# Attention scores of all head pairs laid end to end in 13 groups of 1024 columns

## The chip, the core and the metric

The kernel runs on one core of a Trainium2 chip. The metric is device time in microseconds. Three runs of the kernel before took 338.5, 338.7 and 338.97 us (median 338.7). A profile is one further execution; its durations are those of single instructions, and an average over a group of them is called a mean.

## The reference

Causal attention with 16 extra keys and values ("beacons") that every query sees, and behind it a two-layer network with ELU, over all 4608 tokens:

```python
# q, k, v: (8, 8, 576, 64); beacon_k, beacon_v: (8, 8, 16, 64)
k_all = concat([beacon_k, k], axis=2)              # 592 keys
v_all = concat([beacon_v, v], axis=2)
scores = (1/8) * q @ k_all.T                       # keys past the query are masked out
a = exp(scores - max); a /= a.sum(-1)
x = (a @ v_all) -> (8*576, 8*64)                   # tokens x 512
h = x @ w_in                                       # 512 x 2048
g = where(h > 0, h, exp(min(h, 0)) - 1)
out = g @ w_out                                    # 2048 x 512
```

## The kernel before

**Layout.** A batch has 8 heads, held as 4 pairs: the two heads of a pair lie on the two halves of the 128 partitions, so their score matmuls (64 rows each) run side by side in the array. Scores are computed transposed: keys on partitions, in five chunks of 128 (the last has 80), queries along the columns. A chunk keeps only the queries that may see it, from `ilo = [0, 112, 240, 368, 496]` on, so a pair has 576 + 464 + 336 + 208 + 80 = 1664 columns (`ECOLS`). No maximum is subtracted.

**Steps of attention.** All work is written as small functions, called "steps", which `run` calls in the order of one long text, `word.argument.argument`. Each engine takes its instructions in just that order; waits between engines come from the tiles that instructions read and write.

- `S.b.p.g` (line 302): scores of batch b, pair p, group g of 416 columns, into a PSUM tile of two banks, one per head. Four groups per pair.
- `x.b.p.g` (line 312): exponential of that group on ScalarE into the f16 tile `et` of the pair (2 x 1664 columns, six buffers).
- `m.b.p.g` (line 329): VectorE multiplies the triangles on the chunk's diagonal in that group by the 0/1 tile `triu`. Per pair of a batch from 1 on that is one of 224 columns, three of 256 and one of 160 on 80 partitions.
- `D.b.p.n` (line 360): in batches 3 to 7, VectorE adds the key chunks 1 to 4 of a pair up, so that row sums need fewer matmuls.
- `L.b.g` (lines 344 and 374): row sums of half g (pairs 2g and 2g+1), by matmuls with a matrix of ones; four heads at once, each on 32 columns of the array.
- `n.b.g` (lines 406 and 409): 1/sum on ScalarE as exp(-ln(sum)).
- `W.b.g.half` (line 344): products with v; a head's 64 values are made as two halves of 32, each half in its own PSUM tile (576 columns).
- `M.b.g.half` (line 441): VectorE scales a tile of products by 1/sum and writes it to the f16 tile `xT` of the 512 tokens that it belongs to, in two pieces where a batch crosses a tile of tokens.

Batch 0 is done in two parts of its queries (`A`: 256, `B`: the rest), by lines of its own (450, 457).

**Steps of the network.** `F` is x @ w_in (line 477), `e`/`u`/`k` or `e`/`r`/`g` are the ELU (lines 487, 492, 502; 487, 509, 515), `G` and `Q` are the second product (line 524; from the third tile of tokens on line 588, by seven products of quarters in place of eight, with `Z`, `J`, `wt` as its sums), and for the last two tiles of tokens `P`, `K`, `E`, `U`, `V`, `H`, `X` do most of the first product in the same manner (line 658).

**PSUM.** Its eight banks are split in three: `ops` (two tiles of one bank, second product), `hps` (two of one bank, first product) and `S` (two tiles of two banks). All of `S`, `L`, `W` and the transposes `T` of batches 1 and 2 take turns on the two `S` tiles. A tile is free for the next step when its last reader is done.

**Loads.** GpSimd (POOL) issues all loads with a change of type: `lq` (q and k of batches 0 to 2, transposed by `T` on TensorE), `lk` (q or k of batches 3 to 7 to DRAM in bf16; `lt` brings them back transposed, from SyncE's queue), `lv` (v), `wi`, `wo` (weights). `lp` fills the beacon keys. Output rows are stored from SyncE's queue by `s` and `J`.

**Warm-up.** `warm.12` and `wm.n` are matmuls on zeros (lines 207 and 214), 12 of 512 columns and 99 of 128, put between the steps of batch 0.

The tile that holds scores, and the one that holds sums or products, in the code before:

```python
s = sc[b, p, g] = psum.tile([P, 2, 512], FP32, tag="S", name="sc")       # S, 416 of 512 used
t = psum.tile([P, 1024], FP32, tag="S", name=name)[:, 512 - QA:512 - QA + S]   # L, and each half of W
```

with `QA` = 112, the queries that see the first key chunk alone.

Of the kernel before, what the change touches and what calls it, by code (L numbers as in the profile page):

```python
# [8 lines left out]
FP32 = mybir.dt.float32  # L9
FP16 = mybir.dt.float16  # L10
BF16 = mybir.dt.bfloat16
AFT = mybir.ActivationFunctionType
# [5 lines left out]
def kernel(  # L18
# [169 lines left out]
    triu = konst.tile([P, 2, P], FP16)  # L188
# [42 lines left out]
    tps, qkT, sc, ets = {}, {}, {}, {}  # L231
# [5 lines left out]
    @step  # L237
    def tri():
        nc.gpsimd.memset(triu, 1.0)
        nc.gpsimd.affine_select(  # L240
            out=triu, in_=triu, compare_op=ALU.is_ge, fill=0.0, base=0,
            pattern=[[0, 2], [1, P]], channel_multiplier=-1,
        )
# [28 lines left out]
    @step  # L272
    def cb(b, p):
        qkT[b, p] = qks[p]
        src = bkT[:, p, NB * b:NB * (b + 1)]
        nc.vector.tensor_tensor(out=qkT[b, p][:, 1, 0:NB], in0=src, in1=src, op=ALU.max)
# [14 lines left out]
    def S_(b, p, g):  # L291
        if (b, p) not in ets:
            ets[b, p] = attn.tile([P, 2, ECOLS], FP16, tag="et", bufs=6, name="et")
        s = sc[b, p, g] = psum.tile([P, 2, 512], FP32, tag="S", name="sc")
        t = qkT[b, p]
        c0, c1 = GW * g, GW * (g + 1)
        for (j, qa, qe, col) in lays[b]:
            a, e = max(c0, col), min(c1, col + qe - qa)
            if a >= e:
                continue  # L300
            for h in range(2):
                nc.tensor.matmul(  # L302
                    out=s[:, h, a - c0:e - c0],
                    lhsT=t[D * h:D * (h + 1), 1, P * j:P * (j + 1)],
                    rhs=t[D * h:D * (h + 1), 0, NB + qa + a - col:NB + qa + e - col],
                    start=True, stop=True, skip_group_check=True,
                )
    op["S"] = S_

    @step  # L310
    def x(b, p, g):
        nc.scalar.activation(  # L312
            out=ets[b, p][:, :, GW * g:GW * (g + 1)], in_=sc[b, p, g][:, :, 0:GW],
            func=AFT.Exp, bias=0.0, scale=SCALE)

    @step
    def m(b, p, g, eng="v"):

        c0, c1 = GW * g, GW * (g + 1)
        for (j, qa, qe, col) in lays[b]:  # L320
            base = NB if j == 0 else 0
            e = min(qe, ilo[j] + P - base)
            a, e = max(qa, qa + c0 - col), min(e, qa + c1 - col)
            if a >= e:
                continue
            t0 = a - ilo[j] + base
            o = ets[b, p][0:kc[j], :, col + a - qa:col + e - qa]
            if eng == "v":
                nc.vector.tensor_tensor(out=o, in0=o, in1=triu[0:kc[j], :, t0:t0 + e - a], op=ALU.mult)  # L329
            else:  # L330
                nc.gpsimd.affine_select(
                    out=o, in_=o, compare_op=ALU.is_ge, fill=0.0, base=t0,
                    pattern=[[0, 2], [1, e - a]], channel_multiplier=-1)

    def quad(b, g, qa, qe, t, half, first):
# [5 lines left out]
        for n, (j, a, e, c) in enumerate(pcs):  # L341
            for i in range(4):
# [4 lines left out]
                    rhs=ets[b, p][0:kc[j], i % 2, c:c + e - a],  # L347
# [5 lines left out]
    def D_(b, p, n, eng="v"):  # L353

        r_ = presum[b, p] = qks[p % 2].bitcast(FP16)[:, :, 0:S]
        t = ets[b, p]
# [7 lines left out]
    lt, ut, rls = {}, {}, {}  # L364
    QA = ilo[1]

    def quads(b, g, half, name):

        t = psum.tile([P, 1024], FP32, tag="S", name=name)[:, 512 - QA:512 - QA + S]
        if half is None and b >= BD:  # L370
            for a, e in ((0, QA), (QA, S)):
                for i in range(4):
                    k = b, 2 * g + i // 2
                    nc.tensor.matmul(
                        out=t[32 * i:32 * (i + 1), a:e], lhsT=ones,
                        rhs=(presum if a else ets)[k][:, i % 2, a:e],
                        start=True, stop=True, skip_group_check=True)
            return t
        quad(b, g, 0, QA, t[:, 0:QA], half, True)
        quad(b, g, QA, S, t[:, QA:S], half, True)  # L380
        return t

    @step
    def L(b, g):
# [7 lines left out]
        elif g == "B":  # L392
            t = psum.tile([P, 2, 512], FP32, tag="S", name="lt")
            for i in range(2):
                quad(b, i, CUT, S, t[:, i, 0:S - CUT], None, True)
            lt[b, g] = t[:, :, 0:S - CUT]
        else:
            lt[b, g] = quads(b, g, None, "lt")
# [21 lines left out]
    def W(b, g, *i):  # L420
        half = i[-1]
# [9 lines left out]
        else:  # L431
            ut[b, g, half] = quads(b, g, half, "ut")

    def scale_out(b, cc, qa, qe, u, r):

        tok, end = b * S + qa, b * S + qe
        while tok < end:
            k = tok // TT
            to = min(TT * (k + 1), end)
            o = tok - b * S - qa  # L440
            nc.vector.tensor_tensor(  # L441
                out=x_tile(k)[:, cc, tok - TT * k:to - TT * k],
                in0=u[:, o:o + to - tok], in1=r[:, o:o + to - tok], op=ALU.mult)
# [3 lines left out]
    def M(b, g, *i):  # L447
# [12 lines left out]
        else:  # L460
            scale_out(b, 2 * g + i[0], 0, S, ut[b, g, i[0]], rls[b, g][:, 0:S])
# [262 lines left out]
    def lt_(b, x_):  # L724
# [6 lines left out]
        for y in range(2):  # L731
            qkT[b, 2 * x_ + y] = t[:, y, :, :]
# [20 lines left out]
    lq.0.0.0.4 warm.12 lq.0.1.0.4 lq.0.0.4.8 ident wm.27 bt wm.6 T.0.0.0 bk cq.0.0.0 cb.0.2  # L753
    cb.0.1 T.0.1.0 ck.0.1.0 wm.10 S.0.1.0 x.0.1.0 wm.6 T.0.1.1 cb.0.0 ck.0.1.1 T.0.0.1 S.0.0.0
    x.0.0.0 wm.3 S.0.1.1 x.0.1.1 cq.0.0.1 wm.3 T.0.3.0 T.0.2.0 cb.0.3 cq.0.3.0 cq.0.2.0 S.0.0.1
    x.0.0.1 S.0.1.3 x.0.1.3 wm.8 S.0.1.2 x.0.1.2 lq.0.1.4.8 T.0.3.1 S.0.3.0 T.0.2.1 cq.0.3.1
    lq.1.0.0.4 lv.0.0.1 lv.0.2 tri m.0.1.3 x.0.3.0 cq.0.2.1 m.0.3.0 cb.1.1 S.0.0.3 x.0.0.3 wm.6
    S.0.3.3 x.0.3.3 wm.8 S.0.2.0 x.0.2.0 wm.4 S.0.2.2 wm.6 S.0.2.3 x.0.2.2 x.0.2.3 wm.6 S.0.3.2
    x.0.3.2 wm.6 S.0.0.2 x.0.0.2 wi.0 m.0.3.3 m.0.1.0 m.0.0.0 m.0.0.3 m.0.2.0 L.0.A n.0.A
    T.1.0.0 cb.1.0 m.0.3.2 cq.1.0.0 m.0.0.2 W.0.A.0 S.0.2.1 x.0.2.1 W.0.A.1 m.0.2.2 M.0.A.1  # L760
    M.0.A.0 cb.1.2 m.0.2.3 m.0.1.2 S.1.0.2 x.1.0.2 S.0.3.1 x.0.3.1 T.1.1.0 ck.1.1.0 S.1.0.0
    F.0.1 x.1.0.0 S.1.1.0 x.1.1.0 e.0.1 r.0.1 cb.1.3 g.0.1 F.0.3 S.1.0.3 x.1.0.3 L.0.B n.0.B
    lv.0.3.4 lq.1.0.4.8 wi.1 wo.0 W.0.B.0 M.0.B.0 S.1.1.3 e.0.3 u.0.3 x.1.1.3 F.0.0 u.0.0 e.0.0
    W.0.B.1 M.0.B.1 S.1.1.1 x.1.1.1 F.0.2 e.0.2 r.0.2 k.0.0 g.0.2 S.1.0.1 x.1.0.1 S.1.1.2
    x.1.1.2 F.1.1 u.1.1 lq.2.0.0.8 T.1.2.0 ck.1.2.0 e.1.1 T.1.3.0 F.1.4 e.1.4 k.0.3 cq.1.3.0
    r.1.4 g.1.4 m.1.1.2 cb.2.0 S.1.2.0 x.1.2.0 F.1.5 e.1.5 r.1.5 g.1.5 k.1.1 cb.2.1 S.1.2.2
    x.1.2.2 S.1.3.2 x.1.3.2 G.0.0.0 S.1.2.3 x.1.2.3 F.0.7 e.0.7 r.0.7 g.0.7 m.1.0.3 S.1.3.3
    x.1.3.3 S.1.2.1 x.1.2.1 F.0.4 e.0.4 G.0.1.0 S.1.3.0 x.1.3.0 F.0.5 e.0.5 r.0.4 m.1.3.2 g.0.4
    m.1.0.0 r.0.5 cb.2.2 T.2.2.0 ck.2.2.0 T.2.0.0 cq.2.0.0 m.1.2.0 g.0.5 F.1.7 S.2.2.0 x.2.2.0
    e.1.7 r.1.7 m.1.3.0 g.1.7 m.1.0.1 wo.1 G.0.1.1 S.1.3.1 x.1.3.1 S.2.2.2 x.2.2.2 F.1.0 e.1.0  # L770
    u.1.0 T.2.1.0 cq.2.1.0 m.1.0.2 m.1.1.3 m.1.1.1 wt.1.0 m.1.3.3 m.1.1.0 m.1.2.2 m.1.2.3
    m.1.3.1 m.1.2.1 T.2.3.0 ck.2.3.0 F.1.6 e.1.6 G.0.0.1 S.2.0.0 x.2.0.0 S.2.0.1 x.2.0.1 u.1.6
    m.2.2.2 k.1.6 cb.2.3 F.0.6 e.0.6 r.0.6 g.0.6 L.1.0 n.1.0 L.1.1 n.1.1 F.1.3 lv.1.2.3.4 wo.2
    lv.2.2.3.4 lv.1.0.1 W.1.0.1 M.1.0.1 W.1.0.0 M.1.0.0 k.1.0 F.1.2 e.1.2 u.1.3 u.1.2 e.1.3
    W.1.1.0 W.1.1.1 m.2.2.0 M.1.1.0 M.1.1.1 k.1.2 lk.3.0 G.0.0.2 S.2.0.3 x.2.0.3 S.2.0.2 x.2.0.2
    F.2.1 u.2.1 e.2.1 G.0.1.2 S.2.3.0 x.2.3.0 S.2.1.0 x.2.1.0 F.2.11 u.2.11 e.2.11 F.2.13
    S.2.1.2 x.2.1.2 S.2.3.1 x.2.3.1 wo.3 wt.1.1 lp.3.1 k.1.3 G.0.0.3 k.2.11 o.0.0 e.2.13 u.2.13
    k.2.13 H.1.1 F.2.15 u.2.15 e.2.15 S.2.1.1 x.2.1.1 S.2.3.3 H.1.0 G.0.1.3 o.0.1 k.2.15 m.2.0.0
    k.2.1 F.2.5 G.1.0.0 e.2.5 x.2.3.3 F.2.7 u.2.7 e.2.7 k.2.7 S.2.1.3 x.2.1.3 S.2.3.2 u.2.5
    x.2.3.2 G.1.1.0 F.2.3 G.1.0.1 e.2.3 r.2.3 S.2.2.3 x.2.2.3 S.2.2.1 x.2.2.1 g.2.3 m.2.0.1  # L780
    m.2.0.2 m.2.3.2 G.1.1.1 F.2.6 u.2.6 F.2.0 e.2.6 k.2.6 m.2.1.3 m.2.2.1 m.2.1.2 u.2.0 m.2.2.3
    m.2.1.1 m.2.3.0 m.2.0.3 k.2.5 m.2.1.0 lk.3.1 lt.3.0 s.0.0 lk.4.0 lv.3.0.1 lv.2.0.1 lp.3.0
    S.3.0.1 S.3.0.0 x.3.0.1 m.3.0.1 m.2.3.1 m.2.3.3 e.2.0 k.2.0 F.2.14 u.2.14 x.3.0.0 G.1.1.2
    F.2.8 e.2.8 e.2.14 G.1.0.2 S.3.0.3 x.3.0.3 S.3.0.2 x.3.0.2 wt.3.0 r.2.8 g.2.8 F.2.9 L.2.1
    n.2.1 W.2.1.1 M.2.1.1 D.3.0.0 F.2.2 u.2.2 e.2.2 W.2.1.0 M.2.1.0 e.2.9 r.2.9 g.2.9 m.3.0.0
    k.2.2 L.2.0 F.2.4 W.2.0.0 n.2.0 M.2.0.0 e.2.4 u.2.4 W.2.0.1 F.2.10 u.2.10 e.2.10 k.2.14
# [130 lines left out]
```

## Time and profile before

| | |
|---|---|
| profiled execution | 338.69 us, of which the span from first to last instruction is 337.0 |
| TensorE clock | 1.000 of full speed |
| line 477, first product | 544 matmuls, busy 119.4 us |
| line 588, second product | 896 matmuls, busy 50.6 + 50.0 + 17.3 us |
| line 312, exponentials | 128 of 128x832, busy 108.4 us, mean 916 ns |
| line 329, masks | 164, busy 37.7 us, mean 267 ns |
| line 441, scaling of products | 56, busy 22.4 us, mean 450 ns |
| lines 406 and 409, 1/sum | 14 each of 576 columns, mean 666 and 686 ns |

A group's busy time counts each moment once, also where its instructions overlap; its mean is the whole duration of one instruction, which starts before the one ahead of it has ended. So busy time divided by the count is less than the mean. Matmuls overlap most: the distance between starts tells more than their duration. In the lists of waits a line reads: engine, line, what it waited for, microseconds in all, times, longest. In the chain of waits and the timeline a line begins with start and length in microseconds, and ends with the number of instructions.

### The profile page before, as it was taken

Reading aid. Unit: us, or ns where it says so; the run is one execution under the profiler, and the core shown is the slowest. Engines: PE = TensorE matmul, PEld = TensorE weight load, DVE = VectorE, ACT = ScalarE, POOL = GpSimd, SP = SyncE. Lnnn points to the kernel's source line nnn. Section 1 sums busy time; section 2 is a strip of 40 time slices with the busy share of each in tenths; the row PEclk is TensorE's granted clock in tenths of the full one; section 3 lists DMA queues with packets and bytes.
Section 4 is the critical chain, followed back from the end, with each engine's and each line's share of the span. In section 5 each row is a group of like instructions: output and inputs, shape, how many; then the busy total and the mean of one; then the engine's idle time right before and its main releaser. Section 6 shows DMA issues by size and latency. Waiting matters only on the chain.

```text
span 337.0 us, 8983 instructions
## 1 busy us (share of the span) xinstructions
PE 329.2 (98%) x3643; PEld 210.8 (63%) x3643; DVE 286.0 (85%) x663; ACT 282.7 (84%) x474; POOL 91.2 (27%) x120
## 2 busy tenths in 40 slices
PE   8989999999999999999999999999999999999995
PEld 4767666444545556656565555555656688788684
DVE  2583898666899998999899889999999999999972
ACT  1899989799899988889698989997998688888840
POOL 8786468572015008052411300050000000000000
PEclk9999999999999999999999999999999999999999
DMA  9999999999949909989693914298100110121122
GB/s 115 180 162 189 201 185 166 160 173 154 166 33 126 120 2 110 163 150 144 67 142 84 138 33 107 58 109 68 64 3 31 33 64 31 33 94 33 57 70 93
DMA packets 129082, 34.66 MB, mean 103 GB/s; under 512 B 112913, under 2 KB 127505, under 8 KB 129041
## 3 DMA queue, kind: packets, MB, share of 16 engines
q0 software_dynamic: 94912, 18.49, 67.9%
q1 hardware_dynamic: 33408, 15.34, 21.8%
q8 instruction: 28, 0.46, 0.6%
q10 hardware_dynamic: 720, 0.26, 0.3%
q14 instruction: 14, 0.11, 0.1%
HBM read 37.22 MB, written 15.34 MB: 156 GB/s over the span
## 4 chain that ended last, share of the span: by engine, by line
PE 65%; DVE 20%; ACT 10%; issue 2%; DMA 1%; DVEq 0%; ACTq 0%
PE hps L477 21%; PE ops L588 21%; PE sc L302 6%; DVE gt L502 5%; PE hps L658 5%; ACT et L312 4%; PE ops L524 4%; PE ut L344 4%; DVE xT L441 3%; DVE qk L360 3%; DVE gt L545 2%; DVE et L329 2%; PE w L207 1%; DMA out_dram<-osb 1%; ACT e L487 1%
## 5 line engine op out<-in xcount | busy, mean ns | idle before, releaser
L477 PE MATMUL hps<-xT,w_in 128*128 128x512 f16 (+1 forms) x544 | 119.4, 355 | 0.5
L312 ACT ACTIVATE et<-sc 128x832 f16<-128x832 f32 x128 | 108.4, 916 | 7.1 <-PE sc L302 6.7
L588 PEld LDWEIGHTS <-gt 128*128 128x128 f16 x768 | 73.5, 98 | 19.7 <-issue 2.9
L502 DVE SCALAR_TENSOR_TENSOR gt<-e,r 128x512 f16<-128x512 f32 x108 | 72.9, 685 | 8.9 <-ACT e L487 6.3
L487 ACT ACTIVATE e<-hps 128x512 f32<-128x512 f32 x120 | 74.1, 637 | 6.1 <-PE hps L477 5.5
L477 PEld LDWEIGHTS <-w_in 128*128 128x128 f16 x544 | 49.0, 98 | 44.6 <-issue 8.0
L492 ACT ACTIVATE r<-hps 128x512 f16<-128x512 f32 x108 | 66.9, 637 | 7.1 <-PE hps L477 5.7
L588 PE MATMUL ops<-wt,gt 128*128 128x256 f16 x384 | 50.6, 273 | 0.5 <-DVE osb L604 0.5
L588 PE MATMUL ops<-w_out,gt 128*128 128x256 f16 x384 | 50.0, 273 | 0.0
L329 DVE TENSOR_TENSOR et<-et,triu 128x256 f16<-128x256 f16 (+3 forms) x164 | 37.7, 267 | 3.2 <-ACT et L312 3.2
L149 POOL DMA_DIRECT2D v<-in_v_dram x40 | 34.2, 871 | 12.4 <-issue 7.9
L545 DVE TENSOR_TENSOR gt<-gt 128x1024 f16<-128x1024 f16 x48 | 32.3, 686 | 0.4
L441 DVE TENSOR_TENSOR xT<-ut,rl 128x448 f16<-128x448 f32 (+7 forms) x56 | 22.4, 450 | 4.0 <-PE ut L344 2.8
L344 PEld LDWEIGHTS <-v 128*32 128x32 f16 (+1 forms) x800 | 17.2, 96 | 11.6 <-issue 2.5
L344 PE MATMUL ut<-et,v 128*32 128x464 f16 (+4 forms) x672 | 23.7, 282 | 0.1
L360 DVE TENSOR_TENSOR qk<-qk,et 128x672 f16<-128x672 f16 (+2 forms) x60 | 21.4, 368 | 0.6
L604 DVE TENSOR_TENSOR osb<-ops,sm 128x512 f32<-128x512 f32 x24 | 16.5, 685 | 4.2 <-issue 3.2
L588 PE MATMUL ops<-w_out,s 128*128 128x256 f16 x128 | 17.3, 273 | 0.0
L697 DVE SCALAR_TENSOR_TENSOR gt<-e,r 128x512 f16<-128x512 f32 x24 | 16.1, 686 | 0.6 <-ACT r L687 0.3
L524 PE MATMUL ops<-w_out,gt 128*128 128x512 f16 x64 | 16.5, 380 | 0.0
L588 PEld LDWEIGHTS <-s 128*128 128x128 f16 x128 | 12.4, 98 | 3.2 <-issue 0.2
L509 DVE SCALAR_TENSOR_TENSOR r<-e,one 128x512 f16<-128x512 f32 x12 | 8.3, 690 | 6.9 <-ACT e L487 6.9
(108 smaller groups left out, 395.0 us busy)
## 6 DMA issues: line engine op xcount, KB each, us to landing
out_dram<-osb SPq DMA_DIRECT2D x35, 256.0 KB, 2.2
v<-in_v_dram POOLq DMA_DIRECT2D x24, 128.0 KB, 7.5
scr<-in_q_dram POOLq DMA_DIRECT2D x5, 576.0 KB, 10.0
scr<-in_k_dram POOLq DMA_DIRECT2D x5, 576.0 KB, 14.5
w_in<-in_moe_w_in_dram POOLq DMA_DIRECT2D x16, 128.0 KB, 6.4
w_out<-in_moe_w_out_dram POOLq DMA_DIRECT2D x4, 512.0 KB, 11.4
v<-in_v_dram POOLq DMA_DIRECT2D x8, 112.0 KB, 6.2
v<-in_v_dram POOLq DMA_DIRECT2D x8, 80.0 KB, 6.7
```

The lines of the kernel that those rows point to most:

```text
L149: nc.gpsimd.dma_start(out=vt[b][r0:r0 + n, j, :, :], in_=v[b, :, ilo[j]:ilo[j] + n, :].rearrange("h s d -> s h d"),)
L312: nc.scalar.activation(out=ets[b, p][:, :, GW * g:GW * (g + 1)], in_=sc[b, p, g][:, :, 0:GW], func=AFT.Exp, bias=0.0, scale=SCALE)
L329: nc.vector.tensor_tensor(out=o, in0=o, in1=triu[0:kc[j], :, t0:t0 + e - a], op=ALU.mult)
L344: nc.tensor.matmul(out=t[32 * i:32 * (i + 1), a - qa:e - qa], lhsT=ones[0:kc[j], :] if half is None else v16[0:kc[j], j, h, 32 * half:32 * ...
L360: (nc.vector if eng == "v" else nc.gpsimd).tensor_tensor(out=o, in0=t[0:rows, :, a:e] if n == 0 else o, in1=t[0:rows, :, col:col + e - a], ...
L441: nc.vector.tensor_tensor(out=x_tile(k)[:, cc, tok - TT * k:to - TT * k], in0=u[:, o:o + to - tok], in1=r[:, o:o + to - tok], op=ALU.mult)
L477: nc.tensor.matmul(out=h[:, n_, :], lhsT=w_in16[:, cc, P * fc:P * (fc + 1)], rhs=xt[k][:, cc, a - TT * k:e - TT * k], start=(cc == 0), sto ...
L487: nc.scalar.activation(out=eb[t, i], in_=flat(hp[t, i]), func=AFT.Exp, bias=0.0, scale=1.0)
L492: nc.scalar.activation(out=rb[t, i], in_=flat(hp[t, i]), func=AFT.Relu, bias=0.0, scale=1.0)
L502: nc.vector.scalar_tensor_tensor(out=half(t, i), in0=eb[t, i], scalar=1.0, in1=rb[t, i], op0=ALU.subtract, op1=ALU.min)
L545: (nc.vector if eng == "v" else nc.gpsimd).tensor_tensor(out=o_, in0=a_, in1=b_, op=op_)
L588: nc.tensor.matmul(out=xy[t, n_][:, qd, :], lhsT=lw[:, P * qd:P * (qd + 1)], rhs=wt_[:, c, :], start=(first and qd == 0 and c == 0), stop= ...
```

## The change

For batches 1 to 7 the scores of the four pairs are laid end to end, 4 x 1664 = 6656 columns, and cut in 13 groups of 512 columns per head (1024 with both heads) that pay no heed to where a pair or a key chunk ends. `S.b.g` and `x.b.g` take the place of `S.b.p.g` and `x.b.p.g`; a group may need two pairs' q and k. `et` holds two pairs (three buffers in place of six), and the one group that crosses from the first two pairs to the last two has two exponentials of 512 columns (256 of each head), the others have one of 1024. Batch 0 keeps its groups of 416.

Masks of batches 1 to 7 are two steps per pair in place of four, with three multiplications in place of five: the triangles of chunks 0 and 1 together, those of 2 and 3 together, and that of chunk 4. `triu` gets a third plane for chunk 0, and is read with a stride of zero over the two heads.

In `L` the tile of row sums also takes the products with v of the first 112 queries, both halves. `W.b.g` then makes the other 464 columns of both halves in one tile. `M.b.g.0` scales the first 112 columns of both halves, `M.b.g.1` the rest.

The order text is another from beginning to end (1493 words in place of 1605; warm-up matmuls of 128 columns: 65 in place of 99).

```diff
-    triu = konst.tile([P, 2, P], FP16)
+    triu = konst.tile([P, 3, P], FP16)
...
+        for a, e, base in ((0, 1, NB), (1, 3, 0)):
+            nc.gpsimd.affine_select(
+                out=triu[:, a:e, :], in_=triu[:, a:e, :], compare_op=ALU.is_ge, fill=0.0, base=base,
+                pattern=[[0, e - a], [1, P]], channel_multiplier=-1,
+            )
...
+    EC2 = 2 * ECOLS
+    def et(b, p):
+        if (b, p // 2) not in ets:
+            ets[b, p // 2] = attn.tile([P, 2, EC2], FP16, tag="et", bufs=3, name="et")
+        return ets[b, p // 2][:, :, ECOLS * (p % 2):ECOLS * (p % 2 + 1)]
+    def span(b, g):
+        return (GW * g[1] + ECOLS * g[0], GW) if b == 0 else (512 * g[0], 512)
+    def S_(b, *g):
+        s = sc[b, g] = psum.tile([P, 2, 512], FP32, tag="S", name="sc")
+        c0, w = span(b, g)
+        c1 = c0 + w
+        for p in range(NP):
+            t = qk_of(b, p)
+            for (j, qa, qe, col) in lays[b]:
+                col += ECOLS * p
+                a, e = max(c0, col), min(c1, col + qe - qa)
+                if a >= e:
+                    continue
...
     def x(b, *g):
+        c0, w = span(b, g)
+        for d in range(NP // 2):
+            a, e = max(c0, EC2 * d), min(c0 + w, EC2 * (d + 1))
+            if a < e:
+                et(b, 2 * d)
+                nc.scalar.activation(
+                    out=ets[b, d][:, :, a - EC2 * d:e - EC2 * d], in_=sc[b, g][:, :, a - c0:e - c0],
+                    func=AFT.Exp, bias=0.0, scale=SCALE)
...
+    def m(b, p, g):
+        t = et(b, p)
+        if b > 0:
+            m_ = lambda c: triu[:, c:c + 2, :].unsqueeze(1).broadcast_to([P, 2, 2, P])
+            if g == 0:
+                mask(t[:, :, 0:2 * C1].rearrange("p h (j c) -> p h j c", j=2)[:, :, :, 0:P], m_(0))
+            else:
+                n_ = C3 - C2
+                mask(t[:, :, C2 - n_ + P:C3 + P].rearrange("p h (j c) -> p h j c", j=2)[:, :, :, n_ - P:n_], m_(1))
+                mask(t[0:kc[4], :, C4:ECOLS], triu[0:kc[4], 1:3, 0:ECOLS - C4])
+            return
...
     def L(b, g):
...
-            lt[b, g] = quads(b, g, None, "lt")
+            t = hd[b, g] = psum.tile([P, 1024], FP32, tag="S", name="lt")
+            r_ = lt[b, g] = t[:, 512 - QA:512 - QA + S]
...
+            quad(b, g, 0, QA, r_[:, 0:QA], None, True)
+            for half in range(2):
+                quad(b, g, 0, QA, t[:, 512 - QA * (3 - half):512 - QA * (2 - half)], half, True)
...
     def W(b, g, *i):
...
-            ut[b, g, half] = quads(b, g, half, "ut")
+            t = ut[b, g] = psum.tile([P, 2, 512], FP32, tag="S", name="ut")
+            for half in range(2):
+                quad(b, g, QA, S, t[:, half, 0:S - QA], half, True)
...
     def M(b, g, *i):
...
-            scale_out(b, 2 * g + i[0], 0, S, ut[b, g, i[0]], rls[b, g][:, 0:S])
+            if i[0] == 0:
+                scale_out(b, g, 0, QA, hd[b, g][:, 512 - 3 * QA:512 - QA].rearrange("p (h q) -> p h q", h=2))
+            else:
+                scale_out(b, g, QA, S, ut[b, g][:, :, 0:S - QA])
...
     run("""
-    lq.0.0.0.4 warm.12 lq.0.1.0.4 lq.0.0.4.8 ident wm.27 bt wm.6 T.0.0.0 bk cq.0.0.0 cb.0.2
-    cb.0.1 T.0.1.0 ck.0.1.0 wm.10 S.0.1.0 x.0.1.0 wm.6 T.0.1.1 cb.0.0 ck.0.1.1 T.0.0.1 S.0.0.0
...
+    warm.12 lq.0.0.0.4 lq.0.1.0.4 ident bt bk cb.0.3 T.0.1.0 wm.7 T.0.0.0 ck.0.1.0 lq.0.0.4.8
+    cb.0.1 S.0.1.0 wm.8 T.0.1.1 cq.0.0.0 cb.0.0 T.0.0.1 x.0.1.0 tri lq.0.1.4.8 ck.0.1.1 S.0.0.0
...
+    wo.3 W.1.1 F.1.6 u.1.3 wo.2 G.0.1.2 M.1.1.1 lk.3.0 e.1.6 u.1.6 S.2.8 S.2.6 x.2.8 x.2.6 k.1.3
...
+    k.4.0 D.4.3.3 F.4.11 F.4.8 S.5.3 x.5.3 W.4.0 D.4.2.3 L.4.1 Q.3.56.63 J.3.2.v Q.3.63.70
...
```

## The prediction

> **What bounds the kernel now.** First the page's head, with the busy times.
>
> ```profile
> span 337.0 us, 8983 instructions
> PE 329.2 (98%) x3643; PEld 210.8 (63%) x3643; DVE 286.0 (85%) x663; ACT 282.7 (84%) x474; POOL 91.2 (27%) x120
> ```
>
> TensorE (PE) is busy 98% of the span, but a busy PE need not stream at its rate, so I looked at the distances between its matmuls: first the chain of work that ended last, in order of time, where TensorE runs undisturbed, then the timeline of TensorE where it changes work.
>
> ```profile
> 151.27 1.53 PE ops L588 x14
> 152.80 0.86 PE hps L477 x4
> 154.42 1.73 PE hps L477 x8
> ```
> ```profile
> 109.22 0.93 PE L588 MATMUL ops<-wt,gt 128*128 128x256 f16 x7
> 110.08 0.53 PE L302 MATMUL sc<-kst 64*128 64x128 bf16 x10
> 110.54 1.04 PE L477 MATMUL hps<-xT,w_in 128*128 128x512 f16 x4
> 111.41 0.82 PE L588 MATMUL ops<-wt,gt 128*128 128x256 f16 x6
> ```
>
> Undisturbed, 256 columns take 1.53/14 = 0.109 us and 512 take 1.73/8 = 0.216, or 0.42 ns a column. In the second fence, seven matmuls from 109.22 should hand over at 109.98; the scores start at 110.08, 0.10 late. The ten score matmuls are two groups of 416 columns with both heads at once, 2 x 0.173 us, over at 110.43; line 477 starts at 110.54, 0.11 late. From line 477 to line 588 nothing is lost (110.54 + 0.86 = 111.40). So a change between tile shapes of the array (64 rows for scores, 32 columns for row sums and products with v, 64 columns for transposes, the whole array for the rest) costs about 0.10 us, and a change of work inside one shape costs nothing.
>
> Counting neighbours of different shape among the TensorE words of the order list gives 207 changes, or 207 x 0.102 = 21.1 us. Columns of all forms times 0.42 ns (512 columns 480 times, 256 columns 1192 times, scores 32 x 1664 with two heads at once, sums and products 69,000 with four at once, transposes) give 290 us, and the warm-up matmuls 10.5. With 1.3 us before the first matmul and 4.3 after the last one's start, some 10 of the 337.0 us are left for waiting, about half of them in the first 30 us. TensorE is the bound, and only fewer changes of shape, an earlier start or those waits can give time back.
>
> The waits and two windows say how near the other engines are.
>
> ```profile
> ACT et L312 <- PE sc L302: 6.7, 9, 1.6
> DVE et L329 <- ACT et L312: 3.2, 5, 1.0
> DVE osb L604 <- issue: 3.2, 1, 3.2
> ```
> ```profile
> 100.00:120.00 20.00, 20.00 (x180) 11.96 (x181) 19.79 (x49) 20.00 (x36) 5.61 (x9) 1.00 1.28 104
> 240.00:280.00 40.00, 40.00 (x404) 27.97 (x403) 39.79 (x93) 32.30 (x58) 0.00 (x0) 1.00 0.12 41
> ```
>
> Columns are window, length, busy PE, PEld, DVE, ACT, POOL, clock, DMA share, GB/s. VectorE (DVE) has no room from 240 to 280 us, and DVE and ScalarE (ACT) none from 100 to 120. TensorE still streams there, so they are just fast enough.
>
> In the first 30 us the chain names ScalarE:
>
> ```profile
> 6.14 1.51 PE w L214 x27
> 9.58 0.36 PE sc L302 x5
> 13.14 8.44 ACT et L312 x11
> 25.47 0.98 PE hps L477 x8
> ```
>
> The first score at 9.58 starts a row of exponentials, and line 477 begins at 25.47 because of them.
>
> **The change part by part.** The profiled run took 338.69 us, 1.69 more than its span; the median of the runs is 338.7, so sums against one hold for the other.
>
> *Changes of shape.* Batches 1 to 7 have 91 score groups in place of 112, and products with v are one word per half (14 in place of 28). The new order list, counted the same way, has 180 changes: 56 from full array to scores in place of 67, 58 back in place of 70, 12 to products in place of 22. 27 x 0.102 = 2.75 us saved. Every one lies on the bounding engine. Columns stay the same (1664 per pair, 464 + 112 per product).
>
> *Score pieces.* 13 groups a batch still make 32 pieces a batch, but three are 16, 48 and 32 columns wide. The narrowest row is 80 columns (line 344, 80x80), handed over after 33 ns like its columns. Bounds: nothing, or 33 ns for each short piece, 7 x (3 x 33 - 40) = 0.4 us. I take 0.2, the middle, as no row is that narrow. The Trainium skill, "TensorE: Matmul & The Clock Gate", section "Wait — 56ns, not 53.3ns?", says that starts never come closer than about 25 ns however few the columns; by that, as an estimate, the sum would have 7 x (75 - 40) = 0.25 us, and no run here shows it.
>
> *Exponentials.* From 832 to 1152 columns line 312 and the copies of line 280 go from 900 to 1131 ns less a fixed part, about 0.8 ns a column. In a row 13 take 10.12 us in the timeline (0.78 each, from 11.47), so 1024 columns take some 0.93 to 1.07. Per batch: 16 x 0.78 = 12.5 before; 12 x 0.94 and 2 x 0.51 (the group that crosses the two tiles) = 12.3 after. ScalarE saves 1 to 3 us, off the path but for the stretches above.
>
> *Masks.* 140 multiplications become 84: two of 512 columns and one of 160 per pair, in place of 224, three of 256 and 160. At line 329's busy mean of 37.7/164 = 0.23 us, 140 are 32 us. Line 641 has 128x512 f16 at 0.42 us; so 56 x 0.42 + 28 x 0.2 = 29 us, or less in a row. If the broadcast mask halved the rate, line 515's 0.69 us for 512 columns applies: 56 x 0.27 = 15 us more. I take the saving, 3 us: innermost the mask still steps through 128 neighbouring columns, as in line 329's own rows. Cover: TensorE's stream. Without it, 12 us more on VectorE.
>
> *Scaling of the products.* Forms of line 441 go from 284 ns (128 columns) to 620 (448): 1.05 ns a column and 0.15 fixed. 56 instructions become 42 with the same columns: 0.5 to 2.1 us less on VectorE, covered in the same way.
>
> *PSUM tiles.* Per half, three tiles of the ring of two that scores use become two, and 21 groups fall away: 154 allocations in batches 1 to 7 become 91 + 28 = 119. Against that, the tile with the sums now also holds the products of the first 112 columns: it is free only after line 409 (0.69 us) and a scaling on VectorE (224 columns, about 0.38), where line 406 freed it before. Queued behind a score group that waits for it are all later matmuls. Bounds: no wait, or 14 x 1.1 = 15 us. I take zero, since between line 374 at 220.88 and the next score at 222.82 the old order already left 1.9 us, about what the new hold needs.
>
> *Start.* The 27 warm-up matmuls ahead of the first beacon transpose go (1.5 us of the chain), and the identity is built ahead of the third pair of loads. The first transpose needs the first k load, issued at 2.19 with 5.1 us to landing, so 7.3 in place of 8.4 us, and the chain of exponentials starts about 1 us earlier; but one exponential more stands ahead of the first Ln, and groups are longer (0.16). In all 34 warm-up matmuls of 53 ns fall away. Bounds: 1.8 us gained, or 1 lost if loads come later (the third pair moves behind the identity, 0.7 us on POOL; the fourth behind two mask builds of up to 0.4 each in place of none). I take 0.7 gained.
>
> *Loads.* POOL takes w_out's last quarter before the third, and batch 7's and 6's scratch copies (2.3 us of POOL each) ahead of batch 2's v; SP's transposes move with their batches, with output stores behind them. The bytes ahead of batch 1's v are about the same (8.3 against 8.6 MB in the kernel's types), landed at some 53 us and needed from 55. Bounds: nothing, or 1 us where products wait for w_out. I take 0.2.
>
> *Waits left.* About half of the 10 us come after 30 us. The lighter VectorE can take some of them: bounds 0 and 3; I take 0.4, as the order is new and has waits of its own.
>
> Sum: 338.7 - 2.75 + 0.2 - 0.7 + 0.2 - 0.4 = 335.2 us.
>
> **The rivals.** *More than forecast:* the start gives its whole 1.8 and VectorE's relief 2.5 of the waits: 338.7 - 2.75 - 1.8 - 2.5 = 331.6. For it speaks that all three engines get less to do; against it, the DMA queues are full until 44 us.
>
> *The gain is eaten:* changes of shape vanish, but TensorE then waits at the same places for ScalarE or VectorE, which is likely where those have no room (60 of 337 us), above all if the broadcast masks run at half rate: 12 us more, a quarter of it in such stretches, 3 us: 338.7 - 3.3 + 3 = 338.4. Against it: both engines issue fewer instructions.
>
> *Slower:* the held sums tile. If a score group stands within the new 1.1 us of hold, TensorE stops for what is left. At 14 tiles the 3.5 us gained are gone at 0.25 us each, and from 0.3 each the kernel is slower; at 0.5 it takes 335.2 + 7 = 342. For it: the ring has two tiles, and longer exponentials (0.16 us each) free the other later. Against it: 35 fewer allocations. The Trainium skill, "Perfetto Trace Analysis", section "Optimizing Scalar/DVE Operations", speaks for this rival: where these engines aren't full but make others wait, smaller instructions let work end sooner. The trace shows both cases, full stretches and free ones.
>
> **How the numbers follow.** Forecast 0.55 (333.3 to 336.6), more 0.14, eaten 0.14 (half of it within 0.2%), slower 0.17. A measurement of this kernel tells 0.2%, 0.7 us, from no change. Faster 0.55 + 0.14 + 0.07 = 0.76, same 0.07, slower 0.17. The range leaves out half of "more" and the upper half of "slower": 332.0 to 340.5; the likeliest case alone spans 333.3 to 336.6.
>
> **What would show it.** Right: about 27 fewer gaps of 0.1 us on TensorE around line 302's successor, TensorE busy near 326 us, line 477 first at 24.5 to 25.5 us, masks of 512 columns near 0.42 us, no new wait of TensorE for VectorE. Wrong: masks near 0.69; weight loads of the scores waiting for the scaling that frees the sums tile; gaps over 0.3 us ahead of scores or of w_out's products.

## The result, and the profile after

The changed kernel took 343.1 us (median of four runs, 341.1 to 344.7) where the kernel before took 338.8: 1.013 times as long, 95% interval 1.008 to 1.018. The forecast was 335.2 with 332.0 to 340.5 as its range. A further nine runs of the same kernel, beside others of the kernel before, had a median of 342.3 (338.9 to 346.4), ratio 1.007 (1.004 to 1.010, the two longest left out). It is slower, and its nine runs differ by up to 7.5 us, where those of the kernel before, beside the runs of all experiments, stay within 2 us in each set but for three of 87 (341.7, 469 and 829 us).

The profiled execution took 344.72 us, a span of 342.9; it is the longest of the four. The head of its page, and two of the costliest groups:

```profile
span 342.9 us, 8825 instructions
PE 327.0 (95%) x3609; PEld 210.7 (61%) x3609; DVE 282.8 (82%) x593; ACT 282.9 (83%) x460; POOL 89.4 (26%) x121
```
```profile
L336 ACT ACTIVATE et<-sc 128x1024 f16<-128x1024 f32 (+2 forms) x114 | 104.8, 969 | 11.7 <-PE sc L321 11.5
L341 DVE TENSOR_TENSOR et<-et,triu 128x512 f16<-128x512 f16 (+4 forms) x108 | 31.7, 333 | 1.7 <-ACT et L336 1.6
```

TensorE has 2.2 us less of busy time and VectorE 3.2; the masks take 6.0 us less (37.7 to 31.7) and the exponentials 3.6 (108.4 to 104.8), but ScalarE as a whole is busy as long as before (282.9 us, 282.7 before). The two stretches in which VectorE and ScalarE had no room have some now, and one window is new, the third:

```profile
100.00:120.00 20.00, 19.95 (x192) 11.05 (x190) 19.49 (x42) 19.36 (x31) 9.78 (x12) 1.00 1.26 91
240.00:280.00 40.00, 39.53 (x355) 26.69 (x353) 37.93 (x84) 30.93 (x55) 0.00 (x0) 1.00 0.12 41
30.00:40.00 10.00, 7.13 (x101) 4.73 (x100) 2.72 (x5) 4.79 (x7) 8.11 (x10) 0.83 1.15 188
```

From 30 to 40 us TensorE is busy for 7.13 us in place of 9.75, and its granted clock is 0.83. The list of waits, TensorE alone (its first six lines but the third), says what it waited for:

```profile
PE sc L321 <- issue: 4.4, 1, 4.4
PE sc L321 <- ACT e L522: 1.9, 1, 1.9
...
PE ua L378 <- issue: 0.9, 1, 0.9
PE sc L321 <- ACT et L336: 0.7, 1, 0.7
PE ut L378 <- issue: 0.6, 1, 0.6
```

Three of these are "issue": no tile, no load and no other engine that the profile shows held TensorE up. The timeline of TensorE shows two of the three, where they stand. (The second line of the list, 1.9 us put down to ScalarE, is a stop at 175.86 us, which Theory II takes up.)

```profile
21.11 0.68 PE L378 MATMUL ua<-et,v 128*32 128x256 f16 x25
22.66 0.56 PE L378 MATMUL ua<-et,v 128*32 128x256 f16 x23 [0.87 <-issue]
...
27.04 1.25 PE L378 MATMUL ub<-et,v 128*32 128x320 f16 x40
28.21 0.25 PE L321 MATMUL sc<-qk 64*128 64x192 bf16 x1
32.84 0.58 PE L321 MATMUL sc<-qk 64*128 64x192 bf16 x3 [4.38 <-issue]
```

The first falls between the 25th and the 26th of 48 matmuls of one step, the second between the first and the second of four matmuls of one score group (S.1.4), whose operands are the same tiles. The chain of waits after it shows the lower clock: eight matmuls of 256 columns, 0.98 us elsewhere in this chain, take 1.82.

```profile
28.47 4.38 issue
32.84 0.58 PE sc L321 x3
33.43 1.82 PE hps L512 x8
...
52.64 0.98 PE hps L512 x8
```

What the forecast rested on can be read from the same trace. A change of tile shape still costs 0.10 us: seven matmuls of 0.109 from 169.91 should hand over at 170.67, and the scores start at 170.77. Over all changes away from the whole array the median is 0.098 us in both traces.

```profile
169.91 0.93 PE L623 MATMUL ops<-wt,gt 128*128 128x256 f16 x7
170.77 0.62 PE L321 MATMUL sc<-kst 64*128 64x224 bf16 x14
```

TensorE's time in both traces can be taken apart into columns at 0.417 ns each (undisturbed matmuls of 512 columns start 216 ns apart and those of 256 columns 109, so 256 columns more cost 107 ns), warm-up matmuls at the same rate, changes of shape by their count at 0.102 us, and all else ("waits", with what a lower clock adds). 5.6 us ahead of the first matmul and behind the last one's start are the same in all.

```
us                        before   changed   difference
columns                   286.5    286.5      0.0
warm-up matmuls             7.8      6.0     -1.8
changes of tile shape      21.1     18.4     -2.7   (207 and 180 of them)
waits and lower clock      16.0     26.4    +10.4
```

So the change did what it was costed at, 27 changes of shape fewer for 2.7 us, and 10.4 us of waits came in. The stops named above are 8.4 of them by this account (4.55, 1.03, 0.77 for the three of "issue", 2.05 for the scores at 175.86), the lower clock some 1.2 (0.84 in the eight matmuls, the rest in the transposes behind them).

### The profile page after: what moved, and what is told of

Its sections match the earlier page's. It is cut to its first block, busy times and chain, and to the rows that moved or that the text cites. A ratio compares the mean times of both kernels' runs of the same rounds, so it can differ in the third digit from the quotient of the medians.

```text
span 342.9 us, 8825 instructions
## 1 busy us (share of the span) xinstructions
PE 327.0 (95%) x3609; PEld 210.7 (61%) x3609; DVE 282.8 (82%) x593; ACT 282.9 (83%) x460; POOL 89.4 (26%) x121
## 4 chain that ended last, share of the span: by engine, by line
PE 65%; ACT 15%; DVE 13%; issue 5%; DMA 1%; ACTq 0%; DVEq 0%
PE ops L623 23%; PE hps L512 20%; ACT et L336 7%; PE hps L693 5%; PE sc L321 5%; PE ut L378 4%; ACT e L522 4%; ACT r L527 3%; DVE gt L537 3%; PE ops L559 2%; DVE qk L394 2%; DVE gt L550 1%; DVE r L544 1%; PE lt L378 1%; DVE et L341 1%
## 5 line engine op out<-in xcount | busy, mean ns | idle before, releaser
L336 ACT ACTIVATE et<-sc 128x1024 f16<-128x1024 f32 (+2 forms) x114 | 104.8, 969 | 11.7 <-PE sc L321 11.5
L522 ACT ACTIVATE e<-hps 128x512 f32<-128x512 f32 x120 | 71.9, 612 | 8.7 <-PE hps L512 7.9
L512 PEld LDWEIGHTS <-w_in 128*128 128x128 f16 x544 | 50.0, 98 | 43.5 <-issue 6.1
L527 ACT ACTIVATE r<-hps 128x512 f16<-128x512 f32 x108 | 65.4, 614 | 7.3 <-PE hps L512 5.1
L623 PE MATMUL ops<-w_out,gt 128*128 128x256 f16 x384 | 49.2, 273 | 0.0
L149 POOL DMA_DIRECT2D v<-in_v_dram x40 | 35.2, 922 | 5.8 <-issue 2.1
L341 DVE TENSOR_TENSOR et<-et,triu 128x512 f16<-128x512 f16 (+4 forms) x108 | 31.7, 333 | 1.7 <-ACT et L336 1.6
L378 PE MATMUL ut<-et,v 128*32 128x464 f16 (+3 forms) x560 | 21.2, 296 | 0.8 <-issue 0.6
L472 DVE TENSOR_TENSOR xT<-ut,rl 128x672 f16<-128x672 f32 (+12 forms) x26 | 16.4, 671 | 2.7 <-PE ut L378 2.1
L559 PE MATMUL ops<-w_out,gt 128*128 128x512 f16 x64 | 16.1, 380 | 0.0
L703 ACT COPY kst<-hps 128x512 f32<-128x512 f32 x18 | 10.5, 592 | 6.1 <-PE hps L693 4.8
```

What stands on the lines that cost most here:

```text
L149: nc.gpsimd.dma_start(out=vt[b][r0:r0 + n, j, :, :], in_=v[b, :, ilo[j]:ilo[j] + n, :].rearrange("h s d -> s h d"),)
L336: nc.scalar.activation(out=ets[b, d][:, :, a - EC2 * d:e - EC2 * d], in_=sc[b, g][:, :, a - c0:e - c0], func=AFT.Exp, bias=0.0, scale=SCALE)
L341: nc.vector.tensor_tensor(out=o, in0=o, in1=i, op=ALU.mult)
L378: nc.tensor.matmul(out=t[32 * i:32 * (i + 1), a - qa:e - qa], lhsT=ones[0:kc[j], :] if half is None else v16[0:kc[j], j, h, 32 * half:32 * ...
L512: nc.tensor.matmul(out=h[:, n_, :], lhsT=w_in16[:, cc, P * fc:P * (fc + 1)], rhs=xt[k][:, cc, a - TT * k:e - TT * k], start=(cc == 0), sto ...
L522: nc.scalar.activation(out=eb[t, i], in_=flat(hp[t, i]), func=AFT.Exp, bias=0.0, scale=1.0)
```

## The experiments

**Theory I, instructions come late.** Counted from 0 in the order of their starts, those of its sequencer (waits and branches) among them, TensorE's instruction after each of the three stops is number 705, 961 and 1985: each number 193 of a block of 256. The trace has a DMA queue of its own for instructions (q8) with 28 transfers of 16,384 bytes, and TensorE's 7,252 instructions are 28 blocks of 256 and 84 more. After each of the three stops TensorE goes on 1.27 to 1.38 us after the end of one of these transfers; in the kernel before, the smallest such distance is 2.13 us, and no stop of this kind is seen. The rival: the stops belong to the steps in which they stand.

The first test is the kernel unchanged, again:

> The changed kernel as it is. Theory I (instructions arrive late): TensorE stops again ahead of its instruction number 961, the 193rd of a block of 256, which is the second matmul of score group S.1.4, and as it waits there for a 16 KB fetch whose start depends on how full the DMA queues are, the length of the stop is not the same: 1 to 5 us; the whole 341 to 345 us. Rival (a wait that belongs to the scores of batch 1, for a tile, a load or another engine): a stop of 4.4 us, the same within 0.3 us.

343.45 us (339.8 to 344.6), 1.013 (1.007 to 1.019). The stop stood ahead of the same instruction and was another in length, 2.5 us in the list of waits:

```profile
28.79 0.25 PE L321 MATMUL sc<-qk 64*128 64x192 bf16 x1
31.57 0.58 PE L321 MATMUL sc<-qk 64*128 64x192 bf16 x3 [2.52 <-issue]
```

Then the block boundaries were moved by half a block, with nothing else in the work but the size of warm-up matmuls, in the changed kernel (e2) and in the kernel before (e3):

```diff
-        for _ in range(n):
+        for _ in range(76):
             nc.tensor.matmul(
-                out=w0, lhsT=zero[0:rows, 0:P], rhs=zero[0:rows, :], start=True, stop=True, skip_group_check=True)
+                out=w0[:, 0:80], lhsT=zero[0:rows, 0:P], rhs=zero[0:rows, 0:80], start=True, stop=True,
+                skip_group_check=True)
```

> The 12 first warm-up matmuls of 512 columns become 76 of 80 columns: 6,080 columns in place of 6,144, but 128 more instructions on TensorE's queue (each matmul with its weight load), so every later block boundary falls half a block earlier in the work. Theory I: the stop of 4.4 us in S.1.4 is gone, and so are those of 1.0 us at 22.7 and 66.7 us; the boundaries now fall at work that the changed kernel did at 19.9, 26.4, 36.9, 47.2 us, and the only block used up quickly is the one from 19.9 to 26.4 (5.4 us without its stop; a fetch that starts 2.5 to 4 us after it is asked for, takes 0.95 and is followed by 1.3 needs 4.8 to 6.3): a stop of 0 to 1 us there. Total 343.1 - 4.4 - 1.2 (clock after the stop) - 1.9 + 0 to 1 = 335.6 to 336.6, 338 if the fetches are late. Rival (a wait of S.1.4's own): the stop stays between the same two matmuls, 343 +- 1.

339.05 us (337.4 to 340.2), ratio to before 1.001 (0.9995 to 1.0034): 4.4 us won by 64 matmuls more, against e1, which ran beside it. All three stops of "issue" are gone; S.1.4 runs its four matmuls in a row. But 335.6 to 336.6 was expected, 338 with late fetches, and 1 to 3.4 us of it stayed out. TensorE, no longer held up, comes to the first product of the network ahead of its weights:

```profile
30.16 0.39 PE L322 MATMUL sc<-qk 64*128 64x192 bf16 x4
```
```profile
PE hps L513 <- DMA w_in<-in_moe_w_in_dram: 1.6, 1, 1.6
PE w L207 <- DVE lo L174: 1.3, 1, 1.3
```

(The first fence is from its timeline, the second from its list of waits; with this edit all lines stand one further down, so L322 is the changed kernel's L321.) The second of these waits is in every kernel here.

> The same edit in the kernel before, which has no such stop. Theory I: half a block further its instructions from the 577th to the 833rd of the old count are used up in 4.4 us (20.4 to 24.9), while a fetch needs 2.7 + 0.95 + 1.3 = 4.9 at that place if it starts as late as it did there before, and up to 10 if as late as in the changed kernel: a stop of 0.5 to 5 us appears near 25 us, and the kernel takes 339.3 to 344. Rival (the boundaries are nothing): no stop, 338.8 +- 0.4.

338.81 us, 1.0005 (0.998 to 1.003): a miss. No stop appeared and no time was lost, which is what the rival had said. The fetch for the boundary near 25 us started 1.6 us after the boundary ahead of it was crossed, not 2.7, and ended 1.9 us ahead of the work; one for the boundary at 32.3 us started 4.7 us after and ended 1.3 us ahead, and TensorE wasn't stopped there either (the gap of 0.3 us near it stands 11 instructions ahead of the boundary, and the waits put it down to VectorE's xT). If Theory I holds, a boundary in a dense place is not enough: its fetch must also start late. This run alone would not have told the theory from its rival.

The sharpest form of the test moves the boundaries by 8 matmuls only (the 12 first warm-up matmuls as 20 of 307 columns, an edit as above):

> The changed kernel with its first 12 warm-up matmuls of 512 columns cut in 20 of 307 (6,140 columns in place of 6,144): 8 matmuls, 16 instructions more on TensorE's queue ahead of all else. Theory I in its sharpest form: each stop moves to the work that stands 8 matmuls earlier. The one in S.1.4, between its first matmul and the three after it, goes into the 40 matmuls of W.0.B.0 (the group ahead), 33 of them ahead of it and 7 behind, and all four matmuls of S.1.4 follow one another; the one in the products of W.0.A.1, 25 and 23 matmuls, becomes 17 and 31; the one in W.1.1, 28 and 12, becomes 20 and 20. The long one lasts 0 to 4.5 us as before, by how late its fetch starts, and the whole stays at 340 to 345. Rival (the half-block edit cured something else by chance, the stops belong to their steps): they stay where they were.

The timeline has two stops where they were forecast, to the matmul (17 and 31; 33 and 7; S.1.4 in one), each again ahead of number 193 of its block:

```profile
21.82 0.54 PE L379 MATMUL ua<-et,v 128*32 128x256 f16 x17
23.13 0.65 PE L379 MATMUL ua<-et,v 128*32 128x144 f16 x31 [0.77 <-issue]
...
27.40 1.20 PE L379 MATMUL ub<-et,v 128*32 128x320 f16 x33
29.31 0.31 PE L379 MATMUL ub<-et,v 128*32 128x208 f16 x7 [0.71 <-issue]
29.55 0.39 PE L322 MATMUL sc<-qk 64*128 64x192 bf16 x4
```

In W.1.1 the 40 matmuls ran through, since that block had come just in time, 1.4 us ahead: no stop where one was expected. The whole was 339.95 us (338.7 to 342.2), 1.004 (1.001 to 1.006): just under the 340 expected, for its long stop lasted 0.7 us. Stops that move by exactly 8 matmuls when 16 instructions are put ahead of all else, and are gone with 128, are stops for instructions; the rival is out.

How long the long stop is follows from when its fetch starts. This table, from the records of the instruction queue and of TensorE in the profiled executions, is in us; "late" is the gap beyond the columns of the matmul ahead.

```
                   boundary     fetch            next
                   ahead        starts  ends     instruction  late
before             21.85        24.53   25.47    28.89        -
e8 (below)         22.64        25.03   26.03    28.17        -
e10 (below)        22.63        25.07   26.19    28.14        -
e4 (below)         22.84        26.29   27.58    29.10        0.65
e9                 23.13        27.10   28.05    29.31        0.88
e11 (below)        23.16        28.82   29.77    31.12        2.46
e1                 22.92        29.12   30.02    31.57        2.70
changed            22.66        30.59   31.54    32.84        4.55
```

The fetch itself takes 0.9 to 1.3 us in this table (up to 2.1 elsewhere in these traces), and where TensorE was stopped it went on 1.3 to 1.6 us after it. What differs is its start, 2.4 to 7.9 us after the boundary ahead. In the changed kernel fetches start 1.5 to 7.9 us after it up to 95 us, while most of the loads run (DMA share 1.0 to 2.4 in windows of 10 us up to 70); of the 18 from 100 us on 16 start no later than 0.6 us after it (DMA share 1.25 from 100 to 140, then falling to 0.14). That the loads delay them is argued from this, not shown: the queue of loads is as full during the short delay of e8 (its packets took 163% of the 16 engines' time from 22.7 to 26.1) as during the long one of the changed kernel (136% from 22.7 to 30.5). Why the same program has one start at 2.4 and another at 7.9 isn't settled.

The Trainium skill, "Runtime: NRT & Kernel Launch", section "Instruction fetch mechanics", says that instructions come in blocks of 16 KiB, 256 instructions, over a DMA queue of the sequencer's own, and that crossing a boundary is "mostly hidden". The trace agrees on block and queue, and from 70 us on crossing is hidden here too; ahead of that it cost up to 4.55 us at one boundary.

**Theory II, a transpose behind stores.** The scores at 175.86 read batch 6's q and k. SyncE's queue in the changed kernel has their transposes (lt.6.0, the L763 line) behind three stores, of which the first is listed at 144.88 and the last goes at 163; GpSimd's queue has batch 5's v behind the beacon keys of batch 6 (lp.6.0), which wait for scores:

```profile
144.88 18.56 SPq L642 DMA_DIRECT2D out_dram<-osb  x3
163.55 4.30 SPq L763 DMA_TRANSPOSE qst<-scr  x2
```
```profile
160.06 0.18 POOL L771 MEMSET qst<- 128x96 bf16 x1 [16.23 <-PE sc L321]
160.36 2.15 POOL L772 COPY qst<-bkT 128x32 bf16<-128x32 bf16 x1
162.45 0.53 POOL L144 DMA_DIRECT2D v<-in_beacon_v_dram  x1
```

The scores that free the tile are done at 160.06, so the transposes could have gone 3.5 us earlier. The second of them lands at 175.77, and the scores start 0.09 us after that; the ScalarE instruction to which the list of waits puts this stop down had ended at 175.10. Both loads moved (e4), and the transposes without v (e8; lk.6.1 moves in the text, but on GpSimd's queue it stays ahead of lp.6.0, right behind the same instruction as before):

```diff
-... S.5.6 S.5.4 u.4.8 e.4.11 J.3.3 ... F.4.2 lk.6.1 lt.6.0 ... lp.6.0 ... S.5.7 lv.5
+... S.5.6 S.5.4 lk.6.1 lv.5 lt.6.0 u.4.8 e.4.11 J.3.3 ... F.4.2 ... lp.6.0 ... S.5.7      (e4)
+... S.5.6 S.5.4 lk.6.1 lt.6.0 u.4.8 e.4.11 J.3.3 ... F.4.2 ... lp.6.0 ... S.5.7 lv.5      (e8, e11)
```

> In the changed kernel the load of the transposed q and k of batch 6 (lt.6.0, with lk.6.1) is put ahead of three stores on SyncE's queue, right behind the last scores that read its buffer, and the load of v of batch 5 (lv.5) ahead of the beacon keys of batch 6 (lp.6.0) on GpSimd's queue. Theory II (the stop of 2 us at 173.7 to 175.9, scores of batch 6 waiting, comes from these two orders): the stop is gone or under 0.5 us; 1.5 to 2.1 us less than the changed kernel of the same call, whatever the stop at 28 us does. Rival (another wait stands behind it): the stop stays or moves by under a microsecond, and less than 0.7 us is won.

> The changed kernel with the first half of the loads' edit alone: lt.6.0 (with lk.6.1) ahead of three stores on SyncE's queue, lv.5 left where it was. Theory II in its stronger form (the order on SyncE's queue is the cause): the scores of batch 6 near 174 us wait less than 0.3 us. Rival (the loads of v beside it are the cause): the wait stays over 1 us.

e4: 339.46 us (337.7 to 342.3), 1.003 (1.000 to 1.006); e8: one run, 338.0. In both the stop is gone altogether (scores of batch 6 start 0.1 us after the work ahead of them). In e8 the transposes go right as the tile comes free, with the stores behind:

```profile
155.16 0.18 POOL L771 MEMSET qst<- 128x96 bf16 x1 [16.23 <-PE sc L321]
```
```profile
155.50 2.81 SPq L763 DMA_TRANSPOSE qst<-scr  x2
158.40 12.55 SPq L642 DMA_DIRECT2D out_dram<-osb  x3
```

The order on SyncE's queue was the cause; the loads of v are not needed for it. e4 won 4.0 us where 1.5 to 2.1 were expected, though, and so the two were run against each other once more:

> The changed kernel once more, for how much its runs differ, beside the next one. Theory I (a fetch that is late by chance): 341 to 345 with runs spread over 3 us or more, where those of the kernel before stay within 2. Rival (the spread of the first runs was the chip's): the spread is that of the kernel before.

> The changed kernel with lt.6.0 and lk.6.1 ahead of three stores, now with its time. Up to 135 us both kernels are the same, instruction for instruction, so what the late fetch costs must be spread in the same way, and the medians differ by the stop of batch 6 alone: 1.7 to 2.3 us less than the changed kernel of this call. Rival (the edit also does something ahead of 135 us, as the 4 us between the two loads-earlier and unchanged kernels would have it): 3.5 to 4.5 less.

e10 342.3 (its numbers stand in the first section), e11 340.73 (337.3 to 343.3), 1.002 (0.999 to 1.005): 1.6 us apart, just under the 1.7 to 2.3 expected. With runs that spread over 6 and 7.5 us, these medians alone can't tell 2 us from none. The profiled executions can: e10's (340.2 us) and e8's (338.0) both lack the long stop and any lower clock between 8 and 330 us, and e10's has a stop of 1.97 us ahead of the scores of batch 6, e8's has none. So that stop is worth its 2 us; that the rest of e4's gain was the luck of its fetches is likely, and not shown. The runs of e11 fall apart: four of twelve took 337.3 to 337.7 us, all with a mean granted clock of 0.997 or more; seven of the other eight had 0.988 to 0.995, and these took 339.4 to 343.3. The profiled execution of e11, 341.2 us, has the stop and the clock behind it; that of e8, 338.0, neither.

**Theory III, what is left is the start.**

> The changed kernel with both edits: the block boundaries half a block further and the two loads earlier. Theory: the boundaries' stops and the stop of batch 6 are gone together. The half-block kernel still had 0.74 us of the latter, so 0.5 to 0.7 us less than it: 338.3 to 338.6, no better than the kernel before, since TensorE then comes to the first product of the network (F.0.0) before its weights are there, waits 1.6 to 1.8 us for w_in and works some microseconds at a lower clock. Rival (the two edits' gains add up, 4.4 and 4.0): 335.

338.53 us (337.3 to 340.1), 0.998 (0.997 to 1.000): the time is what the theory had, not all of its reasons. TensorE waits 1.2 us for w_in at F.0.0 (1.6 to 1.8 expected) and 0.8 for w_out, and the granted clock stays at 1.00 between 20 and 40 us, where a lower one was expected. Then the row sums of batch 0's second part went ahead of F.0.0:

```diff
-... M.0.A.1 F.0.0 e.0.0 u.0.0 m.0.3.2 m.0.3.3 L.0.B n.0.B lq.1.0.4.8 W.0.B.0 ...
+... M.0.A.1 m.0.3.2 m.0.3.3 L.0.B n.0.B F.0.0 e.0.0 u.0.0 lq.1.0.4.8 W.0.B.0 ...
```

> As the kernel with both edits, and the row sums of the second part of batch 0 (L.0.B, n.0.B, with their masks m.0.3.2 and m.0.3.3) ahead of F.0.0 in the order. Theory III (what is left of the loss is TensorE coming to F.0.0 before w_in has landed, 1.6 to 1.8 us, with some 0.8 us of lower clock behind it): the wait at F.0.0 falls under 0.5 us, the granted clock stays at 1.00 between 20 and 40 us, and 1.5 to 2.5 us are won on the kernel with both edits: 335.8 to 337. Rival (the start as a whole hangs on loads, whatever the order): L.0.B, W.0.B or the next scores wait as long in its place; within 0.5 us of the kernel with both edits.

338.03 us (336.4 to 339.3), 0.997 (0.995 to 0.998), and a miss: 0.5 us won where 1.5 to 2.5 were expected, and 0.5 is within what the runs of these kernels differ by. F.0.0 no longer waits, but the lines around it do, as the rival said:

```profile
PE tp L268 <- DVE xT L490: 0.7, 1, 0.7
PE tp L268 <- DMA kst<-in_k_dram: 0.7, 2, 0.4
PE sc L322 <- ACT et L337: 0.6, 1, 0.6
PE lt L379 <- ACT et L337: 0.5, 1, 0.5
PE ops L560 <- DMA w_out<-in_moe_w_out_dram: 0.3, 1, 0.3
```

There is also a stop for instructions left in both profiled executions, at number 193 of a block, near 33 us: 0.43 us in e5 and 0.30 in e6, each going on 1.3 to 1.4 us after the fetch's end. e6 is the one version whose interval lies below the kernel before: the change with its block boundaries half a block on, batch 6's transposes ahead of the stores, and the sums first, 0.34% faster than before.

**Theory IV, warm-up matmuls are cover.** The kernel before with the changed kernel's number of warm-up matmuls (and its first 12 as 46 of 134 columns, an edit as in e2):

```diff
-    lq.0.0.0.4 warm.12 ... wm.27 ... wm.6 ... wm.10 ... wm.6 ... wm.3 ... wm.3 ... wm.8 ... wm.6 ... wm.8 ... wm.4 ... wm.6 ... wm.6 ... wm.6
+    lq.0.0.0.4 warm.12 ... wm.27 ... wm.6 ... wm.6 ... wm.3 ... wm.3 ... wm.3 ... wm.3 ... wm.2 ... wm.3 ... wm.2 ... wm.2 ... wm.2 ... wm.3
```

> The kernel before with 65 warm-up matmuls of 128 columns in place of 99, as many as the changed kernel has (the first 12 of 512 columns are cut in 46 of 134, so that the block boundaries stay where they were). It disputes one term of the prediction: what 34 warm-up matmuls fewer, 34 x 53 ns = 1.8 us, bring by themselves. Theory IV (they only fill waits for loads and exponentials of batch 0): the waits grow by as much, 338.5 +- 0.5. Rival (they lie on the path): 1.2 to 1.8 us less, 336.7 to 337.3.

339.22 us (338.1 to 340.6), 1.001 (0.999 to 1.003). Nothing is won, and the trace shows why: by 19.3 us 31 of the 34 matmuls, 1.65 us, have gone, but the same score group starts at 19.29 us in place of 19.36. The rest went into waits, most of it for exponentials. One thing more shows in this trace: from 19.30 to 22.80 us the granted clock is 0.51 (1.00 in the kernel before), and the products that follow start 1.0 us later than before. Three of the twelve runs of e7 have a mean clock of 0.993 or 0.994 (339.9 to 340.6 us), and none of the 29 of the kernel before beside them one below 0.997; the other nine have a median of 339.06, still nothing won.

## Why the prediction was wrong

Two steps failed. "Waits left" put the waits at 0.4 us less, and stops for instructions with a lower clock behind one of them came to 7.5 us more. "Loads" put them at 0.2 us, and they came to 1.7 and 2.05. The terms one by one:

*Changes of shape, -2.75:* right, 2.72. It is the one large term, and it is there in every version.

*Score pieces, +0.2:* 0.4 in the changed kernel's trace. From the two heads' matmuls of 16, 32 and 48 columns to the next it is 28, 28 and 39 ns (medians), 95 ns in place of 40 per batch, and the shortest distance is 25 ns.

*Exponentials, masks, scaling:* the masks ran at full rate (412 ns the median form, 0.42 forecast) and saved 6.0 us where 3 was forecast, the exponentials 3.6 where 1 to 3 (though ScalarE's busy time as a whole did not fall), the scaling 0.4 (22.4 to 22.0 us) where 0.5 to 2.1. No gain from it shows on the path.

*PSUM tiles, nothing:* right. No line of the waits of TensorE's matmuls names the scaling that frees the sums tile, and its weight loads for scores wait 0.2 us for a scaling once (0.4 in the kernel before), so the rival "slower: the held sums tile" had the sign and not the mechanism.

*Start, -0.7:* right as far as it was measured. The first product began at 24.79 in place of 25.40 (24.5 to 25.5 forecast), and in e8, which has no long stop, TensorE had 0.5 us more of columns and changes of shape behind it at 30 us than the kernel before (16.1 against 15.6).

*Loads, +0.2 with bounds 0 and 1:* failed, twice. At 50 us the same count has e8 1.4 us behind (32.8 against 34.2): all else between 30 and 50 us came to 3.2 us where the kernel before had 1.4. The list of waits has the difference in two waits for loads, of w_out at 38.97 and of k at 45.82, the kind that the step named; the kernel before has none of either there.

```profile
PE ops L559 <- DMA w_out<-in_moe_w_out_dram: 1.2, 1, 1.2
PE sc L321 <- ACT et L336: 0.7, 1, 0.7
PE tp L267 <- DMA kst<-in_k_dram: 0.5, 1, 0.5
```

(The waits of e8; that for ScalarE is at about 24 us.) So the term was 1.7 (1.2 and 0.5), not 0.2: time won ahead of a load that isn't there yet is handed back at that load. e6 shows the same for loads, and e7 for exponentials. And "SP's transposes move with their batches, with output stores behind them" had the order the wrong way round for lt.6.0: three stores stood ahead of it, and that cost 2.05 us.

*Waits left, -0.4 with bounds 0 and 3:* failed. It took the waits for a stock that could only shrink or stay. The resource that stopped TensorE, its own instructions, was in the trace of before (the queue q8, with 28 transfers), but no step of the sum asked how fast the new order uses its instructions up: between 22.66 and 28.2 us 256 of them in 5.5 us, where the kernel before took 7.0 there.

With these terms as measured the sum closes on the profiled execution: 335.2 + 1.5 (loads) + 2.0 (lt.6.0) + 7.5 (three stops of 6.35 and 1.2 of lower clock) - 1.7 (the two waits for w_out and k, which a late TensorE no longer has) = 344.5, measured 344.7; the median, 343.1, is of runs whose stops were not all as long. Without the stops and with lt.6.0 in its place it is 335.2 + 1.5 = 336.7; the undisturbed runs of e11 took 337.3 to 337.7. A likely part of the last 0.6 to 1.0 us is in e8's trace, 338.0: it has no long stop, but the other two stand where they stood, 0.36 us ahead of 22.64 and 0.34 ahead of 61.76.

## What to carry to other kernels

A term that is right can still be lost: ask of each microsecond won what TensorE meets next, a load that isn't there, and of each reordered queue what stands ahead of each transfer that work waits for. Where a wait has no releaser, count instructions: a stop that moves with the count is a stop for instructions, and small matmuls packed densely while loads fill the DMA queues were the place for it here. Warm-up matmuls between loads were cover, not cost: taking 34 of them away won nothing, and in three of twelve runs the clock fell.

## What was not expected of the hardware

TensorE can run out of instructions: a 16 KB fetch that takes about 1 us by itself started 7.9 us after the boundary ahead of it, and TensorE stood for 4.55 us. The same program had this stop at 4.55, 2.70 and 0 us in three profiled executions, and this is the likeliest reason that runs of one kernel differ by up to 7.5 us; the executions that were not profiled can't show it.

A stop costs more than its length. After the 2.5 us of e1 the granted clock was 1.00, 0.86, 0.50 and 0.78 in the windows of 4 us from 24 to 40; after 2.46 us in e11 0.89, 0.69 and 1.00 from 28; after the 1.6 us for w_in in e2 0.66 and 0.91 from 24. After the waits of 1.2 us in e5 and e8 it stayed at 1.00. But the length of one wait is not all that counts: in e7 it was 0.51 from 19.30 to 22.80, with no single wait above 0.34 us between 8 and 19 us. The Trainium skill, "TensorE: Matmul & The Clock Gate", section "Part 1: The HAM clock gate (the "warmup" mystery)", has the clock fall to half after an idle window of about 3.4 us; here stops of half that and more were followed by a lower clock, and in e7 short waits in a row were.
